# A softmax sum moved ahead of a copy, two copies swapped between engines, and a shared cast turned round

## Chip, cores, metric

One core of a Trainium2 chip. The metric is the time of one execution in microseconds (us), median over runs.

## The reference

Pooled attention over 8 batches and 8 heads (keys and values averaged over 8 neighbours, 576 to 72), followed by a dense layer with tanh-gelu:

```python
k_p = k.reshape(B, H, Sp, pool, D).mean(axis=3)     # 8, 8, 72, 8, 64
v_p = v.reshape(B, H, Sp, pool, D).mean(axis=3)
attn = softmax(scale * q @ k_p.T)                   # 576 x 72 for each batch and head
x = (attn @ v_p) as 4608 tokens x 512
out = gelu_tanh(x @ w_in) @ w_out                   # 512 -> 2048 -> 512
```

## The kernel before

It works in nine groups of 512 tokens: the first 512 of each batch, and one group of the rest. While TensorE does the dense layers of one group, the other engines prepare the next group's attention; small TensorE jobs of the next group are hung into the matmul sequence by step number ("hooks"). The parts that matter:

```python
def norm(g, j, eng):                       # softmax denominator, reciprocal, product
    e = st[g][("e", j)]
    den = work.tile([128, H], F32, name="den")
    nc.vector.reduce_sum(out=den, in_=e, axis=AX.X)
    ...
# first group, in order
exps(0, 2)
for x in range(2):
    values_half(0, 0, x, [nc.vector, nc.scalar][x], "mm")   # matmuls, then the xT copy
exps(0, 3)
nc.scalar.preload_act_table_set(GELU_SET)
norm(0, 2, nc.vector)
norm(0, 3, nc.vector)
...
def tail_of_attention(hooks, n, va):
    at(hooks, va, xT_tile, n)
    at(hooks, va, nc.scalar.preload_act_table_set, GELU_SET)
    at(hooks, va, values, n, nc.scalar)
# group 1, hooked into the first group's dense layers (128 half-width hidden matmuls, then outputs)
at(hooks, 72, pool, 1, 4, 5)                               # K's last half block
at(hooks, 72, dup_k, 1, 4, 5)
at(hooks, 80, cast_q, 1, 0, 2, nc.gpsimd)
at(hooks, 80, cast_q, 1, 2, 4, nc.vector)
at(hooks, 108, k_transpose_pe, 1, 0, 5)
at(hooks, 108, k_spread, 1, [nc.vector, nc.vector])
for j in range(4):
    at(hooks, [114, 118, 122, 125][j], q_transpose_pe, 1, j, nc.vector, "sc")
for j in range(4):
    at(hooks, [128, 131, 142, 146][j], scores, 1, j)
...
tail_of_attention(hooks, 1, 188)
# later groups: K and q are transposed by DMA, the spread and the scores hooked at
#   56 (k_spread) and [67, 69, 78, 82] (scores)
```

(Cut: the rest of the program, marked by "...".) In words: `pool` averages K or V on VectorE, and `dup_k` copies each pooled block of K beside itself, the last step before TensorE transposes it (five blocks, the fifth of half size). `k_spread` copies the transposed K into a block-diagonal tile. `cast_q` makes bf16 of q and is shared by two engines; TensorE transposes it; `scores` needs K and q. `norm` makes the "softmax product", GpSimd multiplies pooled V by a mask ("mask product"), and `values` multiplies the two into xT, the input of the next group's hidden layer.

The softmax here doesn't subtract the row's maximum and nothing guards it: scores larger than these inputs give would overflow.

## Time and profile before

| | us |
|---|---|
| median of 3 runs, before the prediction | 295.87 (295.57 to 295.91) |
| span of the profiled run | 293.9 |
| TensorE busy | 286.0 (97%) |
| landing of group 1's q (end of the DMA piece in the chain, 18.80 + 13.24) | 32.04 |
| group 1's first scores | 36.26 |
| group 1's hidden layer, after its wait | 53.30 |
| group 2's first scores | 67.32 |

Most lines behind these figures stand in the prediction; the rest are these, TensorE's two first scores, and VectorE's pooling of group 1's K, which runs until 32.27:

```profile
36.26 0.41 PE L214 MATMUL sc<-kbd,qT 128*128 128x144 bf16 x4
...
67.32 0.41 PE L214 MATMUL sc<-kbd,qT 128*128 128x144 bf16 x4
```

```profile
28.47 1.23 DVE L132 TENSOR_TENSOR kv<-kv 128x1024 f32<-128x1024 f32 x1 [4.11 <-DMA kv<-in_k_dram]
...
32.09 0.18 DVE L147 COPY kvb<-kvb 128x64 bf16<-128x64 bf16 x1
```

### The profile page before, as it was taken

How to read it: one execution, taken by the hardware profiler on the slowest of the kernel's cores; microseconds unless marked ns; L12 is line 12 of the kernel's file. 1: busy time of each engine (PE TensorE's matmuls, PEld its weight loads, DVE VectorE, ACT ScalarE, POOL GpSimd, SP SyncE). 2: the span in 40 equal slices, each digit the busy share in tenths (PEclk: the TensorE clock that was granted, in tenths of full speed). 3: DMA queues.
4: the chain of work that ended last, by engine and by line, in shares of the span. 5: the costliest groups of instructions: out<-in, count | busy, mean ns of one | idle time of the engine just before them, and what ended most of it. 6: DMA issues, size and time to landing. Idle time of an engine off the chain costs nothing.

```text
span 293.9 us, 4585 instructions
## 1 busy us (share of the span) xinstructions
PE 286.0 (97%) x1741; PEld 142.7 (49%) x1741; DVE 141.1 (48%) x233; ACT 155.4 (53%) x228; POOL 65.1 (22%) x88
## 2 busy tenths in 40 slices
PE   7889999999999999999999999999999999999996
PEld 3568854445444544454445444544444544444444
DVE  5883769075617570747065806481739100920012
ACT  1475584768067716671576257724673367427500
POOL 3594433221402040114002400240024000100000
PEclk9999999999999999999999999999999999999999
DMA  7999998995599369945994599059944900351012
GB/s 242 357 386 348 382 369 191 342 254 166 129 294 280 116 134 270 265 147 132 263 284 149 126 256 299 7 114 248 285 145 103 170 35 2 81 115 38 0 71 71
DMA packets 73301, 56.32 MB, mean 192 GB/s; under 512 B 45888, under 2 KB 55488, under 8 KB 73280
## 3 DMA queue, kind: packets, MB, share of 16 engines
q1 hardware_dynamic: 73136, 55.98, 70.2%
q8 instruction: 13, 0.21, 0.3%
q10 hardware_dynamic: 144, 0.07, 0.1%
q14 instruction: 8, 0.07, 0.1%
HBM read 36.70 MB, written 9.44 MB: 157 GB/s over the span
## 4 chain that ended last, share of the span: by engine, by line
PE 87%; DMA 7%; SPq 3%; ACT 1%; POOL 1%; issue 0%; DVE 0%; POOLq 0%
PE mm L341 41%; PE mm L325 38%; DMA q_sb<-in_q_dram 5%; DMA w_in_s<-in_moe_w_in_dram 3%; PE xo L291 3%; PE sc L214 2%; PE mm L369 1%; SPq L94 1%; SPq L99 1%; SPq L418 1%; ACT xT L79 1%; PE xo L300 1%; POOL q_b L81 1%; PE mm L336 1%; SPq L92 0%; SPq L111 0%
## 5 line engine op out<-in xcount | busy, mean ns | idle before, releaser
L341 PE MATMUL mm<-w_out_b,gT 128*128 128x512 bf16 x560 | 128.8, 379 | 0.0
L325 PE MATMUL mm<-xT,w_in_b 128*128 128x512 bf16 x512 | 112.0, 379 | 0.3 <-ACT xT L79 0.3
L327 ACT ACTIVATE gT<-mm 128x512 bf16<-128x512 f32 x128 | 76.3, 597 | 38.6 <-PE mm L325 38.6
L341 PEld LDWEIGHTS <-gT 128*128 128x128 bf16 x560 | 52.8, 98 | 59.7 <-issue 2.9
L325 PEld LDWEIGHTS <-w_in_b 128*128 128x128 bf16 x512 | 50.1, 98 | 61.0 <-issue 0.8
L81 DVE COPY osb<-mm 128x512 f32<-128x512 f32 (+2 forms) x37 | 24.2, 658 | 57.6 <-PE mm L341 55.3
L79 ACT CAST xT<-xo 128x1024 bf16<-128x1024 f32 (+1 forms) x18 | 16.6, 967 | 56.9 <-PE xo L291 48.2
L154 POOL TENSOR_TENSOR vbd<-kvb,vmask 128x256 bf16<-128x256 bf16 (+2 forms) x40 | 21.2, 553 | 105.9 <-DVE kvb L134 105.7
L236 DVE TENSOR_REDUCE den<-e 128x8 f32<-128x576 f32 x36 | 26.5, 737 | 36.8 <-ACT e L229 36.8
L132 DVE TENSOR_TENSOR kv<-kv 128x1024 f32<-128x1024 f32 (+3 forms) x19 | 21.9, 1154 | 38.2 <-DMA kv<-in_v_dram 33.3
L229 ACT ACTIVATE e<-sc 128x576 f32<-128x576 f32 x36 | 22.5, 649 | 10.2 <-ACT e L229 5.9
L241 DVE TENSOR_TENSOR eb<-e,r 128x576 bf16<-128x576 f32 x26 | 26.0, 998 | 0.9
L81 POOL CAST q_b<-q_sb 128x2048 bf16<-128x2048 f32 (+2 forms) x9 | 17.6, 1950 | 13.9 <-DMA q_sb<-in_q_dram 13.9
L241 POOL TENSOR_TENSOR eb<-e,r 128x576 bf16<-128x576 f32 x6 | 6.9, 1148 | 58.7 <-ACT e L229 31.4
L336 PE MATMUL mm<-xT,w_in_b 128*128 128x256 bf16 x128 | 15.6, 272 | 0.3 <-DVE xT L81 0.3
L214 PEld LDWEIGHTS <-qT 128*128 128x128 bf16 x128 | 9.9, 98 | 7.3 <-issue 0.8
L214 PE MATMUL sc<-kbd,qT 128*128 128x144 bf16 x128 | 13.1, 226 | 0.4 <-ACT qT L79 0.2
L336 PEld LDWEIGHTS <-w_in_b 128*128 128x128 bf16 x128 | 12.2, 98 | 1.9 <-issue 0.5
L338 ACT ACTIVATE gT<-mm 128x512 bf16<-128x512 f32 x16 | 9.4, 597 | 6.5 <-PE mm L336 6.5
L133 DVE TENSOR_TENSOR kv<-kv 128x512 f32<-128x512 f32 (+3 forms) x19 | 12.4, 651 | 0.6
L536 ACT ACT_TABLE_LOAD x8 | 10.3, 1283 | 0.1
L81 POOL CAST w_in_b<-w_in_s 128x512 bf16<-128x512 f32 (+1 forms) x12 | 9.1, 796 | 1.5 <-DMA w_in_s<-in_moe_w_in_dram 1.5
(58 smaller groups left out, 117.9 us busy)
## 6 DMA issues: line engine op xcount, KB each, us to landing
out_dram<-osb SPq DMA_DIRECT2D x31, 256.0 KB, 6.8
kv<-in_k_dram SPq DMA_DIRECT2D x7, 1024.0 KB, 7.3
q_sb<-in_q_dram SPq DMA_DIRECT2D x7, 1024.0 KB, 5.9
kv<-in_v_dram SPq DMA_DIRECT2D x6, 1024.0 KB, 8.9
w_in_s<-in_moe_w_in_dram SPq DMA_DIRECT2D x8, 512.0 KB, 9.1
w_out_s<-in_moe_w_out_dram SPq DMA_DIRECT2D x4, 1024.0 KB, 13.8
kv<-in_v_dram SPq DMA_DIRECT2D x4, 512.0 KB, 10.1
out_dram<-osb SPq DMA_DIRECT2D x9, 128.0 KB, 2.3
```

The costliest lines, as they stand in the source:

```text
L79: eng.copy(out=out, in_=in_)
L81: eng.tensor_copy(out=out, in_=in_)
L132: add(out=t[:, :, 0:4, :], in0=t[:, :, 0:4, :], in1=t[:, :, 4:8, :], op=ALU.add)
L154: eng.tensor_tensor(out=vbd[p0:128, b, n0:n1, :].rearrange("p (c r) (hh d) -> p c (r hh) d", c=max(m, 1), d=D), in0=kvb[p0:128, 4 + c0:4 + ...
L214: nc.tensor.matmul(out=o, lhsT=qT[:, j, pr, :], rhs=kbd[:, g, pr].rearrange("d hh s -> d (hh s)"), start=True, stop=True)
L229: nc.scalar.activation(out=e.rearrange("p (x h) s -> p x (h s)", x=2), in_=sc[:, :, 0:4 * Sp], func=ACT.Exp, scale=1.0 / 64.0)
L236: nc.vector.reduce_sum(out=den, in_=e, axis=AX.X)
L241: eng.tensor_tensor(out=o.rearrange("p (h s) -> p h s", s=Sp), in0=e, in1=r.unsqueeze(2).to_broadcast([128, H, Sp]), op=ALU.mult)
L325: nc.tensor.matmul(out=hp, lhsT=w_in_b[:, ko, fo * 128:(fo + 1) * 128], rhs=st[g]["xT"][:, ko, :], start=(i == 0), stop=(i == KO - 1))
L327: nc.scalar.activation(out=gT[:, fo, :], in_=hp, func=ACT.Gelu_apprx_tanh)
L336: nc.tensor.matmul(out=hp[:, f, :], lhsT=w_in_b[:, ko, (fo + f) * 128:(fo + f + 1) * 128], rhs=st[g]["xT"][:, ko, c0:c0 + 256], start=(ko ...
L341: nc.tensor.matmul(out=o, lhsT=gT[:, fo, r * 128:(r + 1) * 128], rhs=w_out_b[:, fo, :], start=(fo == 0), stop=(fo == FO - 1))
```

## The change

Its intent is to take three waits off TensorE: before the first group's values, before group 1's q transposes, and before group 1's hidden layer.

```diff
@@ first group
     exps(0, 2)
+    sums(0, 2)                     # the reduce_sum of norm, now by itself
     for x in range(2):
-        values_half(0, 0, x, [nc.vector, nc.scalar][x], "mm")
+        values_half(0, 0, x, [nc.scalar, nc.vector][x], "mm")
@@ group 1
-    at(hooks, 80, cast_q, 1, 0, 2, nc.gpsimd)
-    at(hooks, 80, cast_q, 1, 2, 4, nc.vector)
+    at(hooks, 80, cast_q, 1, 0, 2, nc.vector)
+    at(hooks, 80, cast_q, 1, 2, 4, nc.gpsimd)
-        at(hooks, [114, 118, 122, 125][j], q_transpose_pe, 1, j, nc.vector, "sc")
+        at(hooks, [115, 119, 123, 126][j], q_transpose_pe, 1, j, nc.vector, "sc")
-    tail_of_attention(hooks, 1, 188)
+    tail_of_attention(hooks, 1, 187)
```

(`norm` takes the sum that `sums` left, if there is one.)

More of the change, by code (lines that the diff above doesn't have):

```diff
@@ L231, in exps, with sums @@
         st[g][("e", j)] = e
-    def norm(g, j, eng):
+    def sums(g, j):
         e = st[g][("e", j)]
@@ L236, in norm @@
         nc.vector.reduce_sum(out=den, in_=e, axis=AX.X)
+        st[g][("den", j)] = den
+    def norm(g, j, eng):
+        e = st[g][("e", j)]
+        if ("den", j) not in st[g]:
+            sums(g, j)
+        den = st[g].pop(("den", j))
         r = work.tile([128, H], F32, name="r")
```

## The prediction

> **What bounds the kernel now.** I read the page first, then the busy time by stages, the chain that ended last, and the timelines of single engines around the edited instructions.
>
> The page's first lines, then the table by stages (columns: stretch, its length, busy time of each engine with its instruction count, granted clock, DMA share, GB/s):
>
> ```profile
> span 293.9 us, 4585 instructions
> ...
> PE 286.0 (97%) x1741; PEld 142.7 (49%) x1741; DVE 141.1 (48%) x233; ACT 155.4 (53%) x228; POOL 65.1 (22%) x88
> ```
>
> ```profile
> 16.00:24.00 8.00, 7.05 (x66) 5.42 (x64) 6.34 (x11) 5.35 (x8) 6.77 (x10) 1.00 1.05 386
> 24.00:32.10 8.10, 8.10 (x77) 7.26 (x75) 3.78 (x9) 5.50 (x10) 1.94 (x3) 1.00 1.07 347
> 32.10:36.50 4.40, 4.05 (x48) 3.41 (x46) 2.93 (x8) 1.69 (x4) 3.31 (x4) 1.00 1.05 386
> 36.50:53.30 16.80, 16.48 (x98) 7.46 (x96) 11.70 (x22) 11.36 (x14) 5.66 (x9) 1.00 1.02 292
> 53.30:277.10 223.80, 223.69 (x1279) 103.38 (x1279) 102.09 (x159) 125.08 (x184) 39.06 (x44) 1.00 0.67 169
> ```
>
> TensorE is the bound. From 53.3 us on it has no hole (223.69 of 223.80), so nothing there can be won, and an earlier start of that stretch should move the end by the same amount. All that can be won lies before 53.3: 0.95 us of holes in 16 to 24, none in 24 to 32.1, 0.35 in 32.1 to 36.5, 0.32 at the start of group 1. The change edits exactly these three places. The chain that ended last says what closes them:
>
> ```profile
> 18.80 13.24 DMA q_sb<-in_q_dram
> ...
> 32.19 1.59 POOL q_b L81
> 33.78 0.05 issue
> 33.83 0.40 PE tp L199 x4
> ...
> 51.32 1.94 ACT xT L79 x2
> 53.26 0.04 issue
> 53.30 13.54 PE mm L325 x62
> ```
>
> So there is a fixed point in the middle: group 1's q lands at 32.04 whatever the engines did before (DMA share over 1.0, queue full). Before it, TensorE's holes are cheap, because it would wait there anyway; after it, the 1.59 us GpSimd cast of q blocks the first q transpose.
>
> **What the Trainium skill says.** "SBUF — State Buffer", section "SBUF: two separate sides": VectorE (with two SBUF inputs, or in a 2-port mode) and GpSimd share a port pair under an exclusive lock, and the one that comes second is blocked. The trace agrees: the GpSimd cast of 1024 columns of q takes 1.12 us at 13.06 and 1.58 us at 32.19, beside VectorE's 0.69 us cast that began 0.01 us earlier; the softmax product takes 1.15 us at 18.72 beside GpSimd's casts and 0.76 at 40.08 with GpSimd idle. "VectorE: DVE Perf Modes", section "The perf-mode tier table", has fp32 SBUF copies at 2x and reductions at 1x; the trace has 0.69 us for 1024 columns of the cast and 0.74 for 576 columns of the sum. "ScalarE: Activation LUTs", section "What ACT_TABLE_LOAD costs", gives about 1283 ns; the trace has 1.28 at 18.69 and 37.08. "Perfetto Trace Analysis", section "Optimization Strategy", says to find the gaps of the bounding engine and what blocks each; that is the method here.
>
> **Part 1: sum ahead, xT copies swapped (16 to 24 us).** Nothing is added; two VectorE rows change places, two copies change engines. VectorE's timeline before:
>
> ```profile
> 17.10 0.69 DVE L81 CAST xT<-xo 128x512 bf16<-128x512 f32 x1 [0.69 <-PE xo L270]
> 17.70 0.74 DVE L236 TENSOR_REDUCE den<-e 128x8 f32<-128x576 f32 x1
> 18.48 0.20 DVE L238 RECIPROCAL r<-den 128x8 f32<-128x8 f32 x1
> 18.72 1.15 DVE L241 TENSOR_TENSOR eb<-e,r 128x576 bf16<-128x576 f32 x1
> ```
>
> VectorE idles 0.69 us (16.41 to 17.10) before the copy. The third block's exponential ends at 16.17 + 0.65 = 16.82, so the 0.74 us sum fits at 16.87 to 17.61, nearly all in that hole. The first xT half (ready 17.07) goes to the idle ScalarE: 17.09 to 17.68. VectorE copies the second (ready 17.51) until about 18.22, then reciprocal to 18.4, product requested at 18.4 instead of 18.72. TensorE starts its hidden layer at 17.72 instead of 17.84, but gets the second xT half at 18.26 instead of 18.16: its 16 matmuls end 0.10 later. The transposes that wait for the product start at about 19.79 instead of 19.93, the next at about 21.4 to 21.65 instead of 22.00, and the values after them 0.35 to 0.6 us earlier than 23.03 (which, depends on who gets the shared port). So TensorE reaches group 1's K transposes about 0.35 us or more before its 32.09. There four of five can run; the fifth needs a VectorE copy that ends at 32.09 + 0.18 = 32.27 and hangs on K's DMA. It ran at 32.51, and can run at 32.31. **Part 1 keeps 0.20 us**; the rest is lost in front of that wait.
>
> **Part 2: q cast the other way round (32 to 36.5 us).** TensorE before:
>
> ```profile
> 32.65 0.83 PE L336 MATMUL mm<-xT,w_in_b 128*128 128x256 bf16 x6
> 33.83 0.40 PE L199 MATMUL tp<-identb,q_b 128*128 128x128 bf16 x4 [0.35 <-POOL q_b L81]
> 34.06 0.60 PE L336 MATMUL mm<-xT,w_in_b 128*128 128x256 bf16 x4
> ```
>
> The page counts 0.35 us of idle because it draws a matmul's end late; by starts, the sixth matmul began at about 33.20, one takes 0.109, so the next could start at 33.31 and started at 33.83: 0.52 lost. Blocks 0 and 1 come from GpSimd (ends 33.77), 2 and 3 from VectorE (ends 32.87). Swapped, the first transpose has its data at 32.87, and blocks 2 and 3 (33.77) are wanted at about 34.5. The hooks one step later put a seventh matmul ahead of it and take one out after block 3; the sum of work is the same. New checks: the second transpose also needs the K spread (33.41, wanted 33.9); the first scores need the buffer of the third transposes (copied by about 35.41, wanted 35.5: tight). **Part 2 gives 0.51 us**, together 0.71 at the first scores.
>
> **Does it survive to 53.3?** From the scores on, last gelu, table load, exponentials, sums, products, V pooling, mask products and values follow one another without a free-running transfer in the way: the weights' casts are ready at least 0.4 us before use, and V pooling (45.83, would be 45.1) follows the last product without a wait in the trace, V's first half having landed at 44.2 by the trace's semaphore records. So 0.71 passes on.
>
> **Part 3: values of group 1 one step earlier.** One 0.216 us matmul moves behind the values, to cover the wait for the xT copies (51.32 to 53.26). But the last small matmul of the values already waits for a GpSimd product that ends at 50.32; TensorE comes 0.22 earlier and waits there. **Worth 0.04 us**, not 0.22.
>
> Sum: 0.20 + 0.51 + 0.04 = 0.75 us; 295.87 - 0.75 = **295.1 us**.
>
> **Rivals.** (a) The port race turns over: at 32.18 VectorE got the lock 0.01 us ahead. If GpSimd goes first, blocks 0 and 1 are ready only 1.1 us later, at about 33.9, and part 2 gives nothing: 295.6. For it: the margin. Against it: both starts hang on the same DMA, which the change leaves alone, and three runs agree within 0.34 us. (b) Group 2's first scores take the gain back: K's DMA transpose lands at 66.51 and its spread ends 67.06, with the scores at 67.4. If those transfers don't move along, 0.35 is lost: 295.5. Against it: the DMAs that lead there are issued behind group 1's products, which move too. (c) Part 1's 0.35 to 0.6 arrives in full, because K's copies aren't what holds: 294.7. Against it: the fifth transpose's wait on that copy stands in the program. (d) Nothing shows, since the xT wait at 53.26 is set by something fixed: 295.8.
>
> **Range and chances.** The effect is 0.25%, the runs scatter by 0.1%, and no rival goes beyond 0.4%. Range 294.8 to 295.6: the sum, less either rival a or b, plus a part of c. Faster by over 2% would take 5.9 us, against 1.6 us of holes in all; slower by 2% would take a new stall of 6 us every time, for which no moved wait is long enough. Chances 0.01, 0.98, 0.01.
>
> **What would show it.** Right: VectorE's sum at about 16.9 in the old hole; TensorE's hole before the q transposes gone, the first of them at about 33.2; a new hole of 0.2 to 0.6 us in front of the fifth K transpose at 32.3; q still landing near 32.0; first scores at about 35.55 (before 36.26); group 1's hidden layer at 52.5 to 52.6 (before 53.30 after the xT wait), a wait of about 0.35 us left there, and no hole after it. Wrong: first scores not earlier than 36.0, a VectorE cast of q over 1 us (rival a), a hole at group 2's scores (b), or a span outside 292.9 to 293.6.

## The result

| | before | changed |
|---|---|---|
| median us (4 runs each) | 295.72 | 295.28 |
| range | 295.51 to 295.91 | 295.13 to 295.82 |
| ratio, 95% interval | | 0.9989 (0.9971 to 1.0006) |

A ratio is the mean time of one kernel's fast runs over that of the other's of the same rounds, so not quite the ratio of the medians. By itself this result does not tell the change from no change. Five rounds on another chip (below) gave 0.9978 (0.9966 to 0.999): a real gain, of about 0.2%.

The changed kernel's page, and its busy time by stages with the columns of the prediction's table:

```profile
span 293.6 us, 4585 instructions
...
PE 286.0 (97%) x1741; PEld 143.1 (49%) x1741; DVE 141.0 (48%) x233; ACT 155.4 (53%) x228; POOL 66.0 (22%) x88
```

```profile
16.00:24.00 8.00, 7.37 (x73) 6.15 (x71) 6.14 (x11) 5.68 (x9) 7.42 (x10) 1.00 1.05 386
24.00:32.10 8.10, 8.10 (x77) 7.18 (x75) 3.37 (x7) 5.60 (x10) 2.08 (x3) 1.00 1.07 347
32.10:36.50 4.40, 4.13 (x46) 3.50 (x45) 3.11 (x9) 1.86 (x5) 3.05 (x4) 1.00 1.05 386
36.50:53.30 16.80, 16.60 (x96) 7.53 (x95) 11.80 (x21) 11.21 (x13) 6.72 (x9) 1.00 1.03 304
53.30:277.10 223.80, 223.47 (x1279) 103.10 (x1278) 102.33 (x159) 124.83 (x184) 38.62 (x44) 1.00 0.67 169
```

The first stage's holes fell from 0.95 to 0.63 us. But the last stretch, which had 0.11 us of holes, now has 0.33: 0.17 in front of group 2's first scores at 67.0, where there was none, and 0.16 at group 5's at 156.8, where the 0.11 had been. (The page draws a matmul's end late. By starts, as all holes are counted from here on, these are 0.33, 0.32 and 0.27.) VectorE's timeline in the first group shows part 1 as planned, the sum in the old hole and the product requested earlier:

```profile
17.04 0.75 DVE L236 TENSOR_REDUCE den<-e 128x8 f32<-128x576 f32 x1 [0.44 <-ACT e L229]
17.72 0.69 DVE L81 CAST xT<-xo 128x512 bf16<-128x512 f32 x1
18.33 0.19 DVE L245 RECIPROCAL r<-den 128x8 f32<-128x8 f32 x1
18.56 0.96 DVE L248 TENSOR_TENSOR eb<-e,r 128x576 bf16<-128x576 f32 x1
```

The timeline around group 1's q, TensorE's rows, shows what came of parts 1 and 2. The fifth K transpose now waits for VectorE's copy of K's last block, and seven hidden matmuls run straight into the q transposes, where 0.5 us had been lost:

```profile
32.43 0.20 PE L180 MATMUL kT<-identb,kvb 64*128 64x64 bf16 x1 [0.27 <-DVE kvb L147]
...
32.56 0.94 PE L343 MATMUL mm<-xT,w_in_b 128*128 128x256 bf16 x7
...
33.33 0.39 PE L199 MATMUL tp<-identb,q_b 128*128 128x128 bf16 x4
```

And the chain that ended last, asked from 46 to 75 us, shows where part of the gain went. Before, from 53.3 us on, it was TensorE alone; now it leads through group 2's keys:

```profile
48.58 9.78 DMA kv<-in_v_dram
...
61.45 0.26 DVE kvb L147
...
63.25 3.11 DMA kTd<-kvb
...
66.62 0.24 DVE kbd L81
66.87 0.14 issue
67.00 0.41 PE sc L214 x4
```

Group 2's K is transposed by a DMA that lands at 63.25 + 3.11 = 66.36; VectorE spreads it until 66.86; the first scores start at 67.00. TensorE stood 0.33 us (its start came 0.55 us after the matmul before it, where 0.22 is the pitch).

**Counted from q's landing.** q lands at another time in every execution: between 32.04 and 33.04 in the 14 profiles, by the traces' semaphore records, with the queue full in front of it. The profile before has the earliest of all; the changed kernel's has 32.24. Part 1 does not move it: 32.24 to 33.04 in the nine profiles with part 1, 32.04 to 32.71 in the five without. So stages are compared by their distance from that landing. For the two kernels:

| us after q's landing | before | changed | moved |
|---|---|---|---|
| fifth K transpose | 0.47 | 0.18 | 0.29 |
| first q transpose | 1.79 | 1.09 | 0.70 |
| first scores | 4.22 | 3.40 | 0.82 |
| group 1's hidden layer after its wait | 21.25 | 20.40 | 0.85 |
| K of group 2 spread | 35.02 | 34.61 | 0.41 |
| group 2's first scores | 35.28 | 34.76 | 0.52 |
| group 2's hidden layer | 50.67 | 50.14 | 0.53 |

0.85 us were won by 53 us, and 0.32 of them given back at 67, because group 2's K was spread only 0.41 us earlier.

### The profile page after: what moved, and what is told of

Read it like the earlier page. It is cut to its first block, busy times and chain, and to the rows that moved or that the text cites. A ratio compares the mean times of both kernels' runs of the same rounds, so it can differ in the third digit from the quotient of the medians.

```text
span 293.6 us, 4585 instructions
## 1 busy us (share of the span) xinstructions
PE 286.0 (97%) x1741; PEld 143.1 (49%) x1741; DVE 141.0 (48%) x233; ACT 155.4 (53%) x228; POOL 66.0 (22%) x88
## 4 chain that ended last, share of the span: by engine, by line
PE 69%; DMA 16%; DVE 9%; SPq 3%; issue 1%; POOL 1%; DVEq 0%; POOLq 0%
PE mm L348 33%; PE mm L332 28%; DMA kv<-in_v_dram 5%; DMA kv<-in_k_dram 5%; DMA q_sb<-in_q_dram 3%; DMA kTd<-kvb 3%; DVE kv L132 2%; PE sc L214 2%; PE xo L298 2%; DVE den L236 2%; DVE eb L248 2%; PE mm L376 1%; DVE kv L133 1%; SPq L99 1%; PE mm L343 1%
## 5 line engine op out<-in xcount | busy, mean ns | idle before, releaser
L81 POOL CAST w_in_b<-w_in_s 128x512 bf16<-128x512 f32 (+1 forms) x12 | 9.7, 847 | 0.9 <-DMA w_in_s<-in_moe_w_in_dram 0.9
```

What stands on the lines that cost most here:

```text
L81: eng.tensor_copy(out=out, in_=in_)
```

## The experiments

**Theory.** The cast of q is what the change is worth; part 1 counts only where TensorE, and not VectorE's pooling behind K's DMA, is last in front of the fifth K transpose; part 3 is worth hundredths; and group 2's K takes some 0.3 us back. **Rivals.** Part 1 or part 3 carries the gain; the hooks, not the cast, carry part 2; what is lost at 67 us is paced by something else than K (the table load, the softmax chain).

The first four runs shared one chip (before: 296.12 median of 9), the other eight another (before: 296.06 of 11, then 296.05 of 12). All were correct and timed in 5 rounds (4 to 6 executions each).

| run | median us | ratio to before (95%) | first scores after q | hidden layer 1 after q | hole at group 2's scores |
|---|---|---|---|---|---|
| p1_sums_swap | 295.80 | 0.9995 (0.9981 to 1.0008) | 4.17 | 21.21 | 0 |
| p2_qcast | 295.56 | 0.9979 (0.9967 to 0.9992) | 3.40 | 20.44 | 0.27 |
| p3_values | 295.70 | 0.9987 (0.9975 to 1.0) | 4.17 | 21.06 | 0.43 |
| p12 | 295.47 | 0.9977 (0.9965 to 0.999) | 3.46 | 20.50 | 0.15 |
| after_again | 295.38 | 0.9978 (0.9966 to 0.999) | 3.43 | 20.39 | 0.53 |
| late_g2 | 294.90 | 0.9963 (0.9951 to 0.9974) | 3.45 | 20.45 | 0 |
| late_all | 294.83 | 0.9962 (0.995 to 0.9974) | 3.42 | 20.40 | 0 |
| late_split | 294.86 | 0.9962 (0.995 to 0.9974) | 3.31 | 20.00 | 0.28 |
| casts_only | 295.58 | 0.9983 (0.997 to 0.9996) | 3.51 | 20.55 | 0.19 |
| b_late_g2 | 295.79 | 0.9993 (0.9979 to 1.0008) | 4.17 | 21.21 | 0 |
| late4_split | 294.56 | 0.9952 (0.9939 to 0.9965) | 3.41 | 20.01 | 0 |
| late4_split_c4 | 294.65 | 0.9954 (0.9941 to 0.9967) | 2.95 | 20.02 | 0 |

(A hole is the step from the matmul before, less 0.22. Some traces lack a few matmul records, which shows as single steps of 0.43 in the middle of runs of equal matmuls; those are not counted.)

**p1_sums_swap: part 1 alone.**

```diff
 changed kernel, with
-    at(hooks, 80, cast_q, 1, 0, 2, nc.vector)     +    ... nc.gpsimd)
-    at(hooks, 80, cast_q, 1, 2, 4, nc.gpsimd)     +    ... nc.vector)
-    [115, 119, 123, 126]                          +    [114, 118, 122, 125]
-    tail_of_attention(hooks, 1, 187)              +    ... 188)
```

> Part 1 alone (sum of the third block ahead of the copy, the two xT copies swapped); q cast and hooks as in the kernel before. All positions counted from the landing of group 1's q, which moves by 0.2 us between runs. My theory: TensorE reaches group 1's K transposes 0.4 to 0.6 us earlier but the fifth of them waits for VectorE's copy behind K's DMA; the wait for GpSimd's q cast (blocks 0 and 1) stays and absorbs even the rest, so the first scores stand at 4.2 us after q's landing as in the kernel before (4.22) and the time is the same within 0.1 us. Rival (the gain of part 1 arrives in full): scores 0.4 to 0.6 earlier, time 0.4 to 0.6 us lower.

Its timeline of TensorE:

```profile
32.65 0.20 PE L180 MATMUL kT<-identb,kvb 64*128 64x64 bf16 x1 [0.68 <-DVE kvb L147]
...
34.20 0.40 PE L199 MATMUL tp<-identb,q_b 128*128 128x128 bf16 x4 [0.59 <-POOL q_b L81]
```

TensorE came 0.7 us too early to the fifth K transpose, waited for VectorE's copy of K, then waited for GpSimd's cast as in the kernel before. First scores at 4.17 (before 4.22). The median is 0.32 us under the kernel before, where 0.1 was expected at most, but the interval holds 1: not distinguishable. The gain of part 1 is absorbed twice over; its rival falls.

**p2_qcast: part 2 alone.**

```diff
 kernel before, with
-    at(hooks, 80, cast_q, 1, 0, 2, nc.gpsimd)     +    ... nc.vector)
-    at(hooks, 80, cast_q, 1, 2, 4, nc.vector)     +    ... nc.gpsimd)
-    [114, 118, 122, 125]                          +    [115, 119, 123, 126]
```

> Part 2 alone (blocks 0 and 1 of group 1's q on VectorE, 2 and 3 on GpSimd, hooks one step later). My theory: first scores about 0.5 to 0.6 us earlier than before (about 3.65 us after q's landing), group 1's hidden layer earlier by the same, and of it 0.2 to 0.3 us given back in front of group 2's first scores, where K's DMA transpose and spread end last; time 0.2 to 0.4 us lower. Rival (port race lost): VectorE's cast of q over 1.5 us, no gain.

First scores at 3.40, just where the whole change has them, and 0.56 us off the median (3.65, and 0.2 to 0.4 us, were expected): part 2 alone has the whole gain, as far as these runs can tell. VectorE's cast took 0.69 us and began 0.06 us before GpSimd's.

**p3_values: part 3 alone.**

```diff
 kernel before, with
-    tail_of_attention(hooks, 1, 188)
+    tail_of_attention(hooks, 1, 187)
```

> Part 3 alone (values of group 1 one step earlier, 187 in place of 188). My theory: the last small values matmul waits for GpSimd's mask product, so the start of group 1's hidden layer stays within 0.1 us of 21.26 us after q's landing; time the same. Rival: the whole matmul is won, 0.2 us earlier.

From first scores to hidden layer it takes 21.06 - 4.17 = 16.89 us; with the values at 188 it is 17.03 to 17.04 in all six such profiles. So 0.15 us alone, and 16.96 to 17.00, that is 0.04 to 0.08, in the changed kernel, where part 2 has gone before. The expectation, within 0.1 us of 21.26, missed: 21.06 is where the rival had it, though 0.05 of the difference comes from the earlier first scores. In the changed kernel VectorE's first softmax product takes 0.86 us in place of 0.76, beside GpSimd's cast of w_out, so the last mask product ends 14.17 us after the first scores and not 14.07: there the wait is longer and part 3 is worth less. Its time is unclear (the interval ends at 1.0), and in its profile K came late and took more back than was won.

**p12: the change without part 3.**

```diff
 changed kernel, with
-    tail_of_attention(hooks, 1, 187)
+    tail_of_attention(hooks, 1, 188)
```

> The changed kernel without part 3 (188). My theory: first scores as in the changed kernel, 3.4 us after q's landing, hidden layer of group 1 at 20.4 to 20.5 us after it, then a hole of about 0.3 us in front of group 2's first scores as in the changed kernel; time within 0.1 us of the changed kernel's, 0.3 to 0.5 us under the kernel before. Together with the first run: part 1 is worth nothing alone and 0.2 us with part 2.

295.47 beside 295.56 for part 2 alone: nothing added by part 1 that these runs can tell. The hole at group 2's scores was 0.15, where 0.3 was expected. In this profile q landed latest of all, at 33.04, and the fifth K transpose stood at 0.24 after it; in p2_qcast, which has no part 1, it stood at 0.18. So VectorE's copy behind K's DMA, not TensorE, was last in both. The expected 0.2 us "with part 2" is not there.

**after_again: the changed kernel beside the next ones.** No edit.

> The changed kernel once more, beside the next three on one chip: 0.3 to 0.5 us under the kernel before, with a hole of about 0.33 us in front of group 2's first scores.

295.38 against 296.06, and the hole at group 2's scores, 0.53 us this time.

**late_g2: group 2's first two scores two steps later.**

```diff
 changed kernel, loop over the later groups
+            d = 2 if n_ == 1 else 0
-                at(hooks, [67, 69, 78, 82][j], scores, n, j)
+                at(hooks, [67 + d, 69 + d, 78, 82][j], scores, n, j)     # exps alike
```

> The changed kernel with the first two scores of group 2 alone two steps (0.43 us of output matmuls) later. If K's DMA transpose and spread are what takes part of the gain back, the hole of 0.33 us in front of group 2's first scores goes and the time falls by about 0.3 us against the changed kernel, to 0.7 us under the kernel before. If something else paces that stretch, for example the table load or the DMA transposes of the attention weights, the hole turns up later, at the values, and the time stays.

TensorE's timeline, with two more output matmuls in front of the scores and no hole:

```profile
66.33 1.24 PE L348 MATMUL mm<-w_out_b,gT 128*128 128x512 bf16 x5
67.40 0.41 PE L214 MATMUL sc<-kbd,qT 128*128 128x144 bf16 x4
```

294.90, which is 0.48 us under after_again, whose hole was 0.53; the two runs' times don't overlap. No hole turned up later: 223.80 of 223.80 us are busy from 53.3 to 277.1. So K of group 2 does take part of the gain back, and nothing else paces that stretch in this profile. The exponentials behind the scores wait for the table load anyway, which ends at 68.42, with the first of them at 68.44.

**late_all: the same for all groups** (`[69, 71, 78, 82]`).

> The same delay for all groups. The kernel before has a hole of its own of 0.27 us at group 5's first scores, the changed one has 0.32 there. Theory: that goes as well, another 0.3 us, about 1.0 us under the kernel before. Rival: the later scores delay the softmax chain and the values wait, no gain over the run before this.

294.83, no gain over late_g2 that shows. The hole of 0.27 us at group 5's scores, which had prompted this run, occurs in some executions only: 3 of the 10 profiles without the delay there have it (0.27, 0.32 and, in casts_only, 1.0 us), late_g2 itself has none. The expected further 0.3 us missed.

**late_split: the second xT copy of group 1 on VectorE.**

```diff
 late_all, with
-            copy(eng, st[g]["xT"]...[:, i], xo[i])
+            copy(eng[i] if isinstance(eng, list) else eng, st[g]["xT"]...[:, i], xo[i])
-    tail_of_attention(hooks, 1, 187)
+    tail_of_attention(hooks, 1, 187, [nc.scalar, nc.vector])
```

> The run before, with the second xT copy of group 1's values on VectorE beside the first on ScalarE, in place of both on ScalarE one after the other. Theory: the wait in front of group 1's hidden layer (0.36 us in the changed kernel) goes, another 0.3 us, about 1.3 us under the kernel before. Rival: K of group 2 is again last, the hole opens at group 2's scores, which have some 0.1 us of slack left after the delay: 0.1 us.

The wait in front of group 1's hidden layer went (20.00 after q, was 20.40), and K of group 2 took it back: a hole of 0.28, time unchanged. Its rival was right.

**casts_only: part 2 without the hooks.**

```diff
 kernel before, with
-    at(hooks, 80, cast_q, 1, 0, 2, nc.gpsimd)     +    ... nc.vector)
-    at(hooks, 80, cast_q, 1, 2, 4, nc.vector)     +    ... nc.gpsimd)
```

> The kernel before with the q cast shared the other way round alone, hooks of the q transposes as before. Theory: the cast is what counts, not the hooks: first scores at 3.4 to 3.5 us after q's landing as with part 2 whole, time within 0.1 us of that run's 0.2% under the kernel before. If the hook shift carried the gain, the first q transpose would wait for VectorE's cast and the first scores stand at 3.8 or later.

First q transpose at 1.09 as with the whole of part 2, first scores at 3.51. The 0.11 us of difference is already there at the fifth K transpose (0.29 after q in place of 0.18; the hooks as before put one matmul fewer between it and the q transposes, and one more after them). So the hooks add nothing visible; the cast carries part 2.

**b_late_g2: control, the delay without the change** (the edit of late_g2 on the kernel before).

> The kernel before with group 2's first two scores two steps later and nothing else: a control. If that delay helps only because the change brings TensorE there early, this gains nothing (within 0.1 us of the kernel before; group 2's scores without a hole, as before). If the delay is good in itself, it gains 0.3 us or more here as well.

295.79 against 296.05: more than the 0.1 us expected, but the interval holds 1, and group 2's scores have no hole in either kernel. The delay pays only once TensorE arrives early.

**late4_split: four steps for group 2, two for the others, and the split copy.**

```diff
 late_split, with
+            d = 4 if n_ == 1 else 2
```

> The changed kernel, the second xT copy on VectorE, first two scores of group 2 four steps later, of the other groups two. With two steps the split copy started group 1's hidden layer 0.4 us earlier and gave 0.28 of it back in front of group 2's scores. Theory: with four steps the hole of 0.28 goes and the time is 0.3 us lower, near 294.5, 1.4 us under the kernel before. Rival: the exponentials, now right behind the table load, become late and the values of group 2 wait.

TensorE around the start of group 1's hidden layer, then the last stage of the table:

```profile
50.78 1.25 PE L348 MATMUL mm<-w_out_b,gT 128*128 128x512 bf16 x5
51.87 2.32 PE L332 MATMUL mm<-xT,w_in_b 128*128 128x512 bf16 x10
```

```profile
53.30:277.10 223.80, 223.80 (x1282) 103.57 (x1280) 102.54 (x159) 125.09 (x184) 38.69 (x44) 1.00 0.67 169
```

Five output matmuls run into the hidden layer without a wait, and the scores of group 2 find K spread. 294.56: 1.5 us under the kernel before and 0.8 under the changed one by medians. The best version, faster than both kernels.

**late4_split_c4: the fifth K transpose five matmuls later.**

```diff
 late4_split, with
-    at(hooks, 108, k_transpose_pe, 1, 0, 5)       +    at(hooks, 108, k_transpose_pe, 1, 0, 4)
-    at(hooks, 108, k_spread, ...)                 +    at(hooks, 113, k_transpose_pe, 1, 4, 5)
-    [115, 119, 123, 126]                          +    at(hooks, 113, k_spread, ...); [117, 120, 123, 126]
```

> The run before, with the fifth K transpose of group 1 and the spread five hidden matmuls later, and the q transposes two, one, none and none steps later. Theory: the wait for K's fifth block (0.3 to 0.6 us) is filled with hidden matmuls, but the first q transpose then waits for VectorE's cast, which ends 0.8 us after q's landing: first scores 0.15 to 0.3 us earlier than 3.4 us after it, and 0.1 to 0.3 us off the time. Rival: nothing, because K of group 2 lands no earlier and takes it back.

First scores came at 2.95, 0.46 earlier, more than expected, and nothing of it reached group 1's hidden layer (20.02 beside 20.01). Not for the reason of the stated rival: group 2 is not yet in play there. The first output matmul waited 0.21 us for GpSimd's cast of w_out, which follows w_out's DMA, and then the first softmax product met that cast on the port that both engines share. GpSimd's casts and VectorE's product, of late4_split_c4:

```profile
38.15 2.03 POOL L81 CAST w_out_b<-w_out_s 128x1024 bf16<-128x1024 f32 x2 [0.53 <-DMA w_out_s<-in_moe_w_out_dram]
```

```profile
39.48 1.30 DVE L248 TENSOR_TENSOR eb<-e,r 128x576 bf16<-128x576 f32 x1
```

and the product of late4_split, whose GpSimd casts end at 37.72 + 2.03 = 39.75, soon after it starts:

```profile
39.52 0.83 DVE L248 TENSOR_TENSOR eb<-e,r 128x576 bf16<-128x576 f32 x1
```

The product took 0.47 us longer behind casts that end at 40.18, and the chain behind it (products, V pooling, mask products, values) came no earlier. This is read from the two traces; no run moved that cast. It would be a second fixed point, set by w_out's landing (5.4 us after q's in both).

## Why the prediction was right or wrong

The time was inside the range: 295.28 where 295.1 was said, a gain of 0.44 us by medians where 0.75 was said. The 0.44 is not distinguishable from none by itself, and that the sum came so near is in part luck, since several of its terms were off in opposite directions. Step by step:

- **What bounds the kernel.** Right: three places before 53.3 us, with the fixed point at q's landing. The page shows the places, and p1_sums_swap that what is won before the fixed point is lost at it.
- **Part 1, 0.20 us kept.** Its mechanism was right, the wait in front of the fifth K transpose and the cap it puts on the gain. Its size was read from a profile in which K and q landed earlier than in any other. There TensorE was last at the fifth transpose (0.47 us after q's landing, VectorE's copy done at 0.23). Of the four other profiles without part 1, casts_only has this too (0.29, the copy done at 0.03); in p2_qcast, p3_values and b_late_g2 the transpose stands at 0.18, 0.21 and 0.22, 0.06 after the copy: VectorE's pooling behind K's DMA is last already. Then part 1 is worth nothing, and p12 against p2_qcast shows nothing. So the term is about 0.2 in two of five executions and 0 in three. What caps it is not the DMA alone: K's main blocks land 3.6 to 3.8 us before q, and VectorE pools without a pause from then until that copy; no run shortened this pooling.
- **Part 2, 0.51 us.** Right in mechanism, its size put too low: alone it moves the first scores from 4.17 to 3.40, by 0.77 us, because with q late the wait for the cast is longer than in the profile that was read. The hooks add nothing that shows.
- **Part 3, 0.04 us and not 0.22.** 0.04 to 0.08 in the changed kernel, but 0.15 alone. The wait for the last mask product does cap it, as said. The size came right by luck: without the 0.10 us by which the changed kernel's first softmax product is slower, which was not foreseen, it would have been nearer 0.15.
- **Sum at group 1's hidden layer, 0.75.** 0.85 measured, in one profile of each kernel: part 1 counted in full there, because the profile before was one with TensorE last.
- **"No hole after it".** Wrong, and this is the step that failed: the sum was carried to the end undiminished. Rival b, given 0.35 us and 295.5, came true, with 0.33 us of hole in the profile. The argument against it was that the DMAs that lead to K are issued behind group 1's products, which move too. They are: q and K of group 2 are issued 0.62 us earlier, counted from the landing of group 1's q. But K's main blocks land only 0.45 earlier, and K is transposed and spread 0.41 earlier, where TensorE is 0.85 earlier and had 0.26 of slack. late_g2 takes just this wait away and gains 0.48 us against the changed kernel; the control b_late_g2 gains nothing that shows.
- **Rival a, the port race.** Did not happen: VectorE's cast began 0.01 to 0.06 us before GpSimd's in all 14 profiles. **Rival c** is excluded by p1_sums_swap, **rival d** by p2_qcast.

Left open: why the load of K's main blocks gives up 0.17 us of its earlier issue (9.92 us to landing, before 9.75; 9.57 to 10.08 over the 14 profiles, so part of it may be scatter), and whether issuing K's DMA transpose ahead of q's would free it. The way from that load to the scores is in the trace. SyncE's records have, in front of the transpose of q, a wait for the very semaphore on which K's load counts, and on which the transpose will count too. In all 14 profiles the transpose is issued 0.07 us after that load lands, 2.3 to 3.0 us after q's cast was done. So K's load appears to hold q's transpose, and that holds K's; no run changed the semaphore. SyncE's timeline of the changed kernel has K's transpose issued only when that of q has been let through, though K's pooled copy was done at 61.71:

```profile
57.45 5.71 SPq L205 DMA_TRANSPOSE qT<-q_b  x1
63.25 1.23 SPq L184 DMA_TRANSPOSE kTd<-kvb  x1
```

1.5 us of waiting in the issue queue; no run tried the other order.

## What to carry to other kernels

Before a gain is carried to the end, list what lands last at each later meeting of the bounding engine with a DMA, with its slack: here 0.85 us met a slack of a quarter of a microsecond, at a place where the page before showed no hole. Moving such a meeting two matmuls later cost nothing here, where the consumer waits for something else anyway (the table load), and returned 0.48 us, beside the 0.68 that the change itself had gained on that chip. And a term read from one profile holds for that profile's DMA landing; compare stages by their distance from the landing before assigning tenths of a microsecond.

## What the Trainium skill lacked or had wrong

- "SBUF — State Buffer", section "SBUF: two separate sides": the exclusive port shows in every run (GpSimd's cast of q took 1.53 to 1.58 us beside VectorE's of 0.69, and 1.12 without one on the same size, so it lost 0.41 to 0.46 us and not the whole 0.69; a softmax product took 1.30 us behind a GpSimd cast, 0.76 alone). What it lacks is what this costs a schedule: making VectorE 0.46 us earlier was worth nothing, since the product then met the cast.
- No page that was read says how far a DMA's landing behind a full queue varies from one execution to the next: 32.04 to 33.04 us for the same transfer in 14 profiles (0.38 of spread is there at the first q load already, 8.46 to 8.84), more than the whole change is worth.
- "DMA: Bandwidth & Descriptors" has what a DMA transpose costs its issuing sequencer only in the comparison table of its part on trn3, by cycles for a number of tiles. It lacks times for this chip: here the issue of q's transpose (128 x 2048) held SyncE's queue for 5.7 us, and the next transpose behind it until 1.5 us after its data was ready.
